# Output products of 288 columns, no masked tail copy and another order of the front, in a kernel that runs a recurrent transformer beside full attention

## The chip, the cores and the metric

The kernel runs on one core of a Trainium2 chip as one program. The metric is the device time of one execution in microseconds (us). Before the change four runs gave 1446.75 to 1453.47 us, with a median of 1451.26 us. Engine names are those of the profile: PE (TensorE, matrix products; PEld is its weight load), DVE (VectorE), ACT (ScalarE), POOL (GpSimd) and SP (SyncE, which here only issues transfers).

## The reference

Two branches read the same input `x` of 2048 tokens with 576 values. Branch A goes through 64 segments of 32 tokens, one after the other, and hands a memory of 8 rows from each segment to the next. Branch B is ordinary attention with 32 heads of 18 values. A gate mixes them.

```python
def _A_ref(x, mem0, Wq, Wk, Wv, Wo, seg_len):       # 32 heads of 128 values, M = 8
    mem = mem0
    for s in range(n_seg):
        h = concatenate([mem, x[:, s * 32:(s + 1) * 32, :]], axis=1)      # 40 rows
        q, k, v = (einsum('btd,dhe->bhte', h, W) for W in (Wq, Wk, Wv))
        scores = where(mask, einsum('bhqe,bhke->bhqk', q, k) * scale, -1e9)
        o = einsum('bhqk,bhke->bhqe', softmax(scores), v)
        o = einsum('bhte,hed->btd', o, Wo)
        mem = o[:, :8, :]
        outs.append(o[:, 8:, :])
g = sigmoid((x * gate_w).sum(-1, keepdims=True))
return g * A(x) + (1 - g) * B(x)                       # B: softmax(q k^T) v wo
```

## The kernel before

**An order written by a planner.** Nothing runs in the order of the source. Each piece of work is an operation added with `add(name, engines, duration, function, dependencies, priority, ...)`; a list scheduler (`Plan.run`, `Plan.choose`) places all of them on PE, DVE, ACT, POOL and SP from stored durations, priorities (`RANKS`) and a list of numbers that disturb them (`TURNS`, one number for each segment), and the instructions are then emitted in that order, which is fixed from then on. Some operations may go to either of two engines. Where PE would have nothing to do, the planner puts in four empty products as filler (`warm`, L891). It also charges PE for instruction blocks of 128 pairs of weight load and matmul (`fetched`). Buffers, PSUM banks among them, are tokens: four banks, `pb`, are shared by all products except the scores of the first three heads of a visit of attention (`sb`) and the attention outputs (`ob`).

**The front.** 16 tiles of `x` (128 tokens each) are loaded (L577), every second by SP, the others by ACT. The 576 values are cut into four blocks of 144, each of which gives 128 values to a main part and 16 to a tail; the four tails together are 64 values, which are copied twice side by side (`xd`, L586). PE transposes each tile in five pieces (L594, L595) into one bank `ptx`. Three copies empty it: 512 columns by DVE (L605), the lower 64 rows of the tail by ACT (L609), and the segment's last rows of the upper 64 by ACT (L613) into `xL`; POOL gathers the rest of `xL` (L621, L625). `wb`, the projection weights of B, comes by SP (L638, L639), after POOL has cleared its tail rows (`zwb`, behind five `kch` buffers). Then follow the projections of B: `pq` (L726, 36 blocks of 512 tokens), `pvb` (L765, 32 blocks), the gate `pgs` (L805). Their results go to SBUF (`stg`, `vt`; six buffers each) and by SP to DRAM (`qtd`, `ktd`, `vgd`), from where attention reads them back. `xtd`, the transposed input, is stored by SP (L689, L690) in two transfers for each quarter. The weights of the recurrence, `wv`, `wq` and `wk`, come in 12 loads by POOL (L661, L666), each of which is held back until a certain evacuation of the projections is done (`beats`, a list of numbers in `load_weights`; a one-element memset on DVE, L648, is the sign).

**Attention of B.** 512 visits: scores of four heads (L921; `sb`, `sp`), exponentials on ACT (L930, L934), products with the values (L944, `ob`). They are laid beside everything else; 48 may run ahead of the segments, the others are spread over them.

**A segment of A.** The 40 rows are split: 32 (8 of memory and 24 of `x`) go through the chain below, and the projections of the last 8, which no memory enters, are made ahead for 16 segments at once (`last_unit`, L1014, L1018). `ht` holds the transposed rows: four main blocks and two for the tails, number 4 with the tails in partitions 0 to 63 and zeros above, number 5 the other way round, because `wq_t`, `wk_t` and `wv_t` hold two halves of the heads in the two halves of the partitions. The chain of a segment is: six projections `pvv` (L1270), evacuation `tm` (L536 on DVE, L534 on ACT: one helper, `copier`), transposes by DMA, `qk` (L1370), scores `psh` (L1385, L1393), exponentials (L1403), sums `pss`, reciprocals, `prb` (L1437), `pso` (L1459), copies `ot` (L536, L534), and the output product `acc` (L1178). All of it is done in two halves of 16 heads. The output product lays the four blocks of 144 output columns in the four column groups of PE: for each head four matmuls of 32 columns of `ot` by 144 columns of `wo`. Both halves add to one bank. Then the step to the next segment: `obf`, the cast of 128x144 (L1491); `bd` (L1494), the 16 tail columns of each block, repeated and multiplied by a block mask; the fold `pw` (L1513, L1516), small products with pieces of the identity that turn the 8 memory rows into columns; and `ht` (L1526). The late 8 rows of four segments have an output product of their own (`last_out`, 128 matmuls from `otl`), a cast `lbf` (L1553) and a store to `a_dram`.

**The end.** The last products of B (L1682, L1686) are combined with A's rows, read back from `a_dram`, and stored.

Of the kernel before, what the change touches and what calls it, by code (L numbers as in the profile page):

```python
# [57 lines left out]
    4631337, 8646187, 1378870, 7501440, 2920177, 4654182, 7605534, 9845851, 5556687, 7848165, 8138688,  # L58
    4164138, 9631951, 8743530, 8517736, 8416788, 8054394, 26198, 4924923, 6020877, 419892, 4069693, 9961447,
    272705, 2067139, 5598403, 4732882, 1549104, 2438338, 4732220, 2816846, 6717326, 0, 4595530, 1604277,  # L60
    3301672, 3391804, 6451070, 1335116, 2191429, 1816650, 137719, 3868929, 6979129, 7748565, 6565385, 6695724,
    3839835, 1101164, 2930722, 1706253, 5558244, 8554903, 5450599, 6671946, 1219286, 8487400, 306976, 914519,
    2736263, 2428798, 8437421, 1579326, 8783738, 2627635,
# [47 lines left out]
class Plan:  # L111
# [7 lines left out]
    CROWDED = (28.0, 125.0)  # L119
# [256 lines left out]
def kernel(  # L376
# [29 lines left out]
    QC = 512  # L406
# [40 lines left out]
    sel = const.tile([P, M], BF16, name="sel")  # L447
    bmask = const.tile([P, NF, TR], BF16, name="bmask")
# [10 lines left out]
    nc.vector.memset(bmask[:], 0.0)  # L459
# [11 lines left out]
    for j in range(4):  # L471
        r = slice(32 * j, 32 * j + 32)
        nc.vector.tensor_copy(out=sel[r, :], in_=ident[r, 32 * j:32 * j + M])
        nc.vector.memset(bmask[r, j, :], 1.0)
    selm = ident[:, :].rearrange("p (j t) -> p j t", t=32)[:, :, 0:M]
# [3 lines left out]
    xtd = dpool.tile([Dm, S], BF16, name="xtd")  # L479
# [66 lines left out]
    nc.vector.memset(xT[TL:P, NF, :], 0.0)  # L546
# [4 lines left out]
    z_wb = zero("zwb", wb[TL:P, NF, :], 1.6, 0.05)  # L551
    z_xl = [zero("zxl0", xL[TL:P, NF, :], 0.5, 0.2), zero("zxl1", xL[0:TL, NF + 1, :], 0.5, 0.2)]
# [20 lines left out]
    def x_tile(n):  # L573
        def load(e):
# [5 lines left out]
            f"x{n}", "SP" if n % 2 == 0 else "ACT", 0.42, load, prio=0.1, take=("xn",), dmas=1, kb=147  # L580
        )

        def dup(e):
            box["xd", n] = xd = given(pw, "xd", [P, 2, NF, TR], BF16)
            tail = box["xn", n][:, :].rearrange("p (c r) -> p c r", r=RW)[:, :, P:RW]
            nc.vector.tensor_copy(out=xd[:, :, :, :], in_=tail.unsqueeze(1).to_broadcast([P, 2, NF, TR]))  # L586
# [3 lines left out]
        def turn(e):  # L590
            box["ptx", n] = ptx = bank([P, NF + 1, P], BF16, "ptx")
            xn, xd = box["xn", n], box["xd", n]
            for c in range(NF):
                nc.tensor.transpose(out=ptx[:, c, :], in_=xn[:, RW * c:RW * c + P], identity=ident[:, :])  # L594
            nc.tensor.transpose(  # L595
                out=ptx[:, NF, :], in_=xd[:, :, :, :].rearrange("p a c r -> p (a c r)"), identity=ident[:, :]
# [7 lines left out]
            f"xe{n}", "DVE", psum_copy(512, True),  # L604
            lambda e: nc.vector.tensor_copy(out=xT[:, 0:NF, cols], in_=box["ptx", n][:, 0:NF, :]), [tu], prio=0.2,  # L605
        )
        e2 = add(
            f"xf{n}", "ACT", act_time(128),
            lambda e: nc.scalar.copy(out=xT[0:TL, NF, cols], in_=box["ptx", n][0:TL, NF, :]), [tu], prio=0.2,  # L609
        )  # L610

        def third(e):
            nc.scalar.copy(  # L613
                out=xL[TL:P, NF + 1, lc].rearrange("p (s t) -> p s t", t=LO),
                in_=box["ptx", n][TL:P, NF, :].rearrange("p (s t) -> p s t", t=seg)[:, :, last],
            )

        e3 = add(f"xg{n}", "ACT", act_time(32), third, [tu, e1, e2, *z_xl], prio=0.2, give=(("pb", tu, 0),))

        def gather(e):  # L620
            nc.gpsimd.tensor_copy(  # L621
                out=xL[:, 0:NF, lc].rearrange("p c (s t) -> p c s t", t=LO),
                in_=xT[:, 0:NF, cols].rearrange("p c (s t) -> p c s t", t=seg)[:, :, :, last],
            )
            nc.gpsimd.tensor_copy(  # L625
                out=xL[0:TL, NF, lc].rearrange("p (s t) -> p s t", t=LO),
                in_=xT[0:TL, NF, cols].rearrange("p (s t) -> p s t", t=seg)[:, :, last],
            )

        e4 = add(f"xl{n}", "POOL", 0.6, gather, [e1, e2, *z_xl], prio=2.0)  # L630
        xdone.append((e1, e2, e3, e4))
# [4 lines left out]
    def load_wb(c):  # L636
        def fn(e):
            dma(out=wb[:, c, :], in_=rows(B_wqkv, c))  # L638
            dma(out=wb[TR * c:TR * c + TR, NF, :], in_=B_wqkv[RW * c + P:RW * c + RW, :])  # L639

        return add(f"wb{c}", "SP", 0.8, fn, [z_wb], prio=0.14, dmas=2, kb=500)

    wbl = [load_wb(c) for c in range(NF)]
    beats, weight_loads, paced = [], {}, []

# [8 lines left out]
    def load_weights():  # L654
        k = 0
        for w, src, name in ((wv, A_Wv, "wv"), (wq, A_Wq, "wq"), (wk, A_Wk, "wk")):
            w2 = src.rearrange("d h e -> d (h e)")
            weight_loads[name] = []
            for c in range(NF):
                def load_w(e, w=w, w2=w2, c=c):  # L660
# [3 lines left out]
                    for two in range(2):  # L664
                        o = TL * two + TR * c
# [6 lines left out]
                    behind(f"{name}{c}", beats[(12, 16, 18, 23, 26, 30, 34, 38, 43, 48, 53, 57)[k]], lambda w=w, c=c: w[0][0:1, 0, c, 0:1], 3, load_w, [], 3.0)  # L672
# [3 lines left out]
    def load_gw(e):  # L676
        for c in range(NF):
            nc.gpsimd.dma_start(out=gw[:, c:c + 1], in_=gate_w[RW * c:RW * c + P].unsqueeze(1))
            nc.gpsimd.dma_start(
                out=gw[TR * c:TR * c + TR, NF:NF + 1], in_=gate_w[RW * c + P:RW * c + RW].unsqueeze(1)  # L680
            )

    gwl = add("gw", "POOL", 8.0, load_gw, [wbl[-1]], prio=0.9, tail=3.0)

    def store_xt(q):
        c4 = slice(q * QC, (q + 1) * QC)

        def fn(e):
            dma(out=xtd[0:NF * P, c4].rearrange("(c p) t -> p c t", p=P), in_=xT[:, 0:NF, c4])  # L689
            dma(out=xtd[NF * P:Dm, c4], in_=xT[0:TL, NF, c4])  # L690

        deps = [o for n in range(4 * q, 4 * q + 4) for o in xdone[n][:2]]
# [1066 lines left out]
```

## Time and profile before

| what | us |
|---|---|
| median of four runs | 1451.26 |
| the profiled execution | 1453.47 |
| its span, first to last instruction | 1451.7 |
| first projection `pvv` of segment 0 starts | 162.7 |
| first and last `obf` start | 184.5, 1420.7 |
| ACT: exponentials of B (L930, L934) | 743.6 and 305.0 |
| DVE: `tm`, `ot`, `obf`, `bd` (L536, L536, L1491, L1494), one | 0.689, 0.484, 0.307, 0.196 |

A row of the profile names the line, the engine, the operation and "out<-in" by the program's names. "Idle before" is what the engine spent waiting ahead of such an instruction, and the name behind the arrow is what ended that wait; "issue" is a wait for nothing that the profile shows. A timeline row with x16 is 16 instructions that follow each other.

### The profile page before, as it was taken

To read this page: it belongs to the slowest core of one execution; us is meant where nothing else is said; L and a number is where in the kernel's file an instruction comes from. 1 tells how busy PE (TensorE), PEld (TensorE's weight loads), DVE (VectorE), ACT (ScalarE), POOL (GpSimd) and SP (SyncE) were. 2 spreads that over 40 slices of the span, in tenths; PEclk is the share of its full clock that TensorE was granted. 3 is DMA by queue.
4 is the path that set the end of the run, shared out by engine and by line. 5 is a ranking of instruction groups with operands and counts; after the bars stand their busy time and mean duration, and the time that the engine had idled before them with its cause. 6 is when DMAs were issued, how large, how long until landed. Compare 5 with 4: busy or idle time off the path is not lost. (4 is left out here: it accounts for less than half of the span.)

```text
span 1451.7 us, 79317 instructions
## 1 busy us (share of the span) xinstructions
PE 1353.8 (93%) x35682; PEld 747.6 (52%) x35682; DVE 786.6 (54%) x1873; ACT 1094.2 (75%) x1302; POOL 537.6 (37%) x1166
## 2 busy tenths in 40 slices
PE   6789999999999999999999999999999999989998
PEld 4334545555555545555555445555554444444545
DVE  6334555565555455555555554545565554555556
ACT  1357799878788777787777786788769887778884
POOL 5233254334532355322453325343344334421320
PEclk9899999999999999999999999999999999999999
DMA  6895633233333443423333333433334333433335
GB/s 213 274 319 168 154 77 77 59 68 70 87 57 68 59 80 76 72 62 61 79 67 72 66 63 69 76 59 74 62 71 94 53 54 58 69 61 54 53 71 177
DMA packets 343424, 130.79 MB, mean 90 GB/s; under 512 B 296943, under 2 KB 329159, under 8 KB 343083
## 3 DMA queue, kind: packets, MB, share of 16 engines
q1 hardware_dynamic: 314771, 81.20, 28.5%
q0 software_dynamic: 27088, 43.31, 10.7%
q8 instruction: 279, 4.57, 1.3%
q10 hardware_dynamic: 1224, 1.20, 0.3%
q14 instruction: 62, 0.51, 0.1%
HBM read 52.74 MB, written 30.86 MB: 58 GB/s over the span
## 5 line engine op out<-in xcount | busy, mean ns | idle before, releaser
L930 ACT ACTIVATE etb<-sb 128x1536 bf16<-128x1536 f32 x512 | 743.6, 1452 | 229.2 <-PE sp L921 166.1
L536 DVE CAST tm<-pvv 128x512 bf16<-128x512 f32 x343 | 236.4, 689 | 238.3 <-PE pvv L1270 235.5
L1270 PEld LDWEIGHTS <-ht 128*32 128x32 bf16 x7680 | 197.6, 97 | 222.8 <-issue 37.8
L934 ACT ACTIVATE etb<-sp 128x512 bf16<-128x512 f32 x512 | 305.0, 596 | 0.0
L921 PE MATMUL sb<-qch,kch 32*128 32x512 bf16 x1536 | 202.0, 385 | 8.4 <-ACT etb L930 4.1
L944 PE MATMUL ob<-etb,vch 128*32 128x512 bf16 x2048 | 199.5, 384 | 0.3 <-DVE tq L972 0.3
L921 PE MATMUL sp<-qch,kch 32*128 32x512 bf16 x512 | 196.9, 385 | 0.5 <-issue 0.2
L1178 PE MATMUL acc<-wo,ot 128*32 128x144 bf16 x8192 | 169.8, 228 | 15.5 <-issue 12.4
L1178 PEld LDWEIGHTS <-ot 128*32 128x32 bf16 x8192 | 135.3, 97 | 48.9 <-issue 27.0
L1270 PE MATMUL pvv<-wk_m,ht 128*32 128x512 bf16 x2048 | 145.7, 381 | 2.0 <-DVE vl L536 0.7
L1270 PE MATMUL pvv<-wq_m,ht 128*32 128x512 bf16 x2048 | 142.6, 381 | 3.7 <-DVE ht L1526 1.8
L1270 PE MATMUL pvv<-wv_m,ht 128*32 128x512 bf16 x2048 | 144.5, 380 | 0.0
L921 PEld LDWEIGHTS <-kch 32*128 32x128 bf16 x2048 | 55.7, 91 | 144.2 <-issue 122.1
L536 DVE CAST ot<-pso 128x320 bf16<-128x320 f32 x203 | 93.5, 484 | 66.9 <-PE pso L1459 63.5
L1221 POOL COPY ht<-xg 128x96 bf16<-128x96 bf16 x64 | 17.9, 280 | 282.3 <-PE pvv L1270 273.5
L1370 DVE COPY qk<-tt 128x512 bf16<-128x512 bf16 x256 | 77.6, 308 | 39.0 <-DMA tt<-tm 36.3
L840 POOL DMA_DIRECT2D qch<-qtd x120 | 61.1, 516 | 75.6 <-PE sp L921 66.5
L1403 ACT ACTIVATE et<-psh 128x320 bf16<-128x320 f32 x128 | 56.5, 444 | 35.1 <-PE psh L1393 30.7
L1448 DVE TENSOR_TENSOR et<-et,prb 128x320 bf16<-128x320 bf16 x128 | 61.4, 484 | 37.2 <-PE prb L1437 31.8
L840 POOL DMA_DIRECT2D otd<-stage x124 | 62.9, 514 | 45.9 <-DVE stage L987 32.4
L944 PEld LDWEIGHTS <-vch 128*32 128x32 bf16 x2048 | 54.1, 95 | 44.7 <-issue 34.7
L840 POOL DMA_DIRECT2D kch<-ktd x112 | 57.0, 516 | 44.6 <-PE sp L921 37.0
(169 smaller groups left out, 1934.2 us busy)
## 6 DMA issues: line engine op xcount, KB each, us to landing
xl<-qkd SPq DMA_DIRECT2D x64, 128.0 KB
v_sb<-tm SPq DMA_DIRECT2D x256, 32.0 KB
qkd<-vl POOLq DMA_DIRECT2D x48, 128.0 KB, 2.1
wo<-in_A_Wo_dram POOLq DMA_DIRECT2D x4, 1152.0 KB
vgd<-vt SPq DMA_DIRECT2D x32, 128.0 KB
wv_m<-in_A_Wv_dram POOLq DMA_DIRECT2D x4, 1024.0 KB, 7.2
wq_m<-in_A_Wq_dram POOLq DMA_DIRECT2D x4, 1024.0 KB
wk_m<-in_A_Wk_dram POOLq DMA_DIRECT2D x4, 1024.0 KB, 8.3
```

What stands on the lines that cost most here:

```text
L536: nc.vector.tensor_copy(out=out_of(), in_=in_of())
L840: dma(out=rows_, in_=pads) if out else dma(out=pads, in_=rows_)
L921: nc.tensor.matmul(sb[:, j, :] if j < 3 else sp[:, :], lhsT=kc[r, o:o + P], rhs=qt_[r, :], start=True, stop=True, tile_position=(32 * j, 0),)
L930: nc.scalar.activation(out=etb[:, 0:3, :], in_=box["sb", gq, kb][:, :, :], func=ACT.Exp, scale=scale_b)
L934: nc.scalar.activation(out=etb[:, 3, :], in_=box["sp", gq, kb][:, :], func=ACT.Exp, scale=scale_b)
L944: nc.tensor.matmul(ob[32 * j:32 * j + 32, :], lhsT=vc[:, o + 32 * j:o + 32 * j + 32], rhs=etb[:, j, :], start=(kb == 0), stop=(kb == NKB - ...
L1178: nc.tensor.matmul(acc[32 * j:32 * j + 32, :], lhsT=o[:, slot, t0:t0 + CT], rhs=wo[:, h, RW * j:RW * j + RW], start=(first and s_ == 0), s ...
L1221: nc.gpsimd.tensor_copy(out=ht[:, 0:NF, M:CT], in_=xg[:, 0:NF, t])
L1270: nc.tensor.matmul(pv[32 * j:32 * j + 32, :], lhsT=ht[:, cc, :], rhs=rw, start=(c == 0), stop=(c == NF), tile_position=(0, 32 * j), skip_g ...
L1370: eng.tensor_copy(out=opened["qk"][:, hf, a, 0:16 * L].rearrange("p (j i t) -> p j i t", i=4, t=L)[:, :, :, 0:CT], in_=box["tt", s, a, hf] ...
L1403: nc.scalar.activation(out=opened["et", hf][:, :], in_=box["psh", s, hf][:, :], func=ACT.Exp, scale=scale_a)
L1448: nc.vector.tensor_tensor(out=et[:, :], in0=et[:, :], in1=box["prb", s, hf][:, :], op=ALU.mult)
```

## The change

There are four parts, and an order planned anew for all of them.

1. **Output products.** `out_pieces` gets `wide`. Then a head has two matmuls of 288 columns instead of four of 144; heads with an even number write the partitions 0 to 63, those with an odd number 64 to 127. So the bank holds two partial sums, which `halved` adds: two copies of 64x144 to an FP32 tile `sum` (DVE or ACT) and two additions (DVE). It is used for the first half of each segment and for the late rows. The second half stays at 144 columns, has a bank of its own, and `obf` becomes the addition of that bank and `sum`. The four output blocks lie in the order 0, 2, 1, 3 (`SL`).
2. **Tails.** The tails are laid out so that each block has its 16 values twice (32 partitions). `bd` is gone; the fold takes the tail columns from `obf` itself, which is made 16 columns wider, always as 12 matmuls, and the zeros come from multiplying by `keep` when `pw` is evacuated. `xtd` and `xg` carry the doubled tails, so that a transfer each replaces two and three.
3. **Front.** One copy (DVE or ACT) empties `ptx`, and POOL makes the tails of `xL` with two multiplications. The four `sel` copies and the memset of `xT` are gone. The four main loads of `wb` are shared by SP and ACT, ahead of most tiles of `x`.
4. **Later transfers.** The recurrence weights wait for later beats, and the stores of `xtd` wait for beats 60, 63, 65 and 67 (of 68).

```diff
 TURNS = [
-    4631337, 8646187, 1378870, 7501440, 2920177, 4654182, 7605534, 9845851, 5556687, 7848165, 8138688,
+    2111328, 67141, 7494148, 5731960, 1836367, 3235203, 8807839, 6809858, 7066401, 7875931, 2541338, 4628007,
...
-    CROWDED = (28.0, 125.0)
+    CROWDED = (40.0, 112.0)
...
-        nc.vector.tensor_copy(out=sel[r, :], in_=ident[r, 32 * j:32 * j + M])
-        nc.vector.memset(bmask[r, j, :], 1.0)
-    selm = ident[:, :].rearrange("p (j t) -> p j t", t=32)[:, :, 0:M]
+        nc.vector.memset(keep[r.start:r.start + TR, NF:NF + 1], 1.0)
...
+    SL = (0, 2, 1, 3)
...
-    nc.vector.memset(xT[TL:P, NF, :], 0.0)
...
-    z_wb = zero("zwb", wb[TL:P, NF, :], 1.6, 0.05)
+    z_wb = zero("zwb", wb[:, NF, :], 1.6, 0.05)
...
         e1 = add(
-            f"xe{n}", "DVE", psum_copy(512, True),
-            lambda e: nc.vector.tensor_copy(out=xT[:, 0:NF, cols], in_=box["ptx", n][:, 0:NF, :]), [tu], prio=0.2,
+            f"xe{n}", ("DVE", "ACT"), (psum_copy(640, True), act_time(640)),
+            copier(lambda: xT[:, :, cols], lambda: box["ptx", n][:, :, :]), [tu], prio=0.2, give=(("pb", tu, 0),),
         )
...
     def load_wb(c):
-        def fn(e):
-            dma(out=wb[:, c, :], in_=rows(B_wqkv, c))
-            dma(out=wb[TR * c:TR * c + TR, NF, :], in_=B_wqkv[RW * c + P:RW * c + RW, :])
-
-        return add(f"wb{c}", "SP", 0.8, fn, [z_wb], prio=0.14, dmas=2, kb=500)
+        main = add(
+            f"wb{c}", "SP" if c % 2 == 0 else "ACT", 0.42,
+            lambda e: (nc.sync if e == "SP" else nc.scalar).dma_start(out=wb[:, c, :], in_=rows(B_wqkv, c)),
+            [z_wb], prio=0.12, dmas=1, kb=442,
+        )
...
+    BEATS = (20, 24, 27, 30, 33, 36, 40, 45, 49, 53, 57, 60)
...
-                    behind(f"{name}{c}", beats[(12, 16, 18, 23, 26, 30, 34, 38, 43, 48, 53, 57)[k]], lambda w=w, c=c: w[0][0:1, 0, c, 0:1], 3, load_w, [], 3.0)
+                    behind(f"{name}{c}", beats[BEATS[k]], lambda w=w, c=c: w[0][0:1, 0, c, 0:1], 3, load_w, [], 3.0)
...
+    XBEATS = (60, 63, 65, 67)
...
-            dma(out=xtd[0:NF * P, c4].rearrange("(c p) t -> p c t", p=P), in_=xT[:, 0:NF, c4])
-            dma(out=xtd[NF * P:Dm, c4], in_=xT[0:TL, NF, c4])
+            dma(out=xtd[:, c4].rearrange("(c p) t -> p c t", p=P), in_=xT[:, :, c4])
...
-                    for j in range(4):
+                    for j in range(2 if wide else 4):
+                        q = 2 * (s_ % 2) + j if wide else j
+                        n, d = (2 * RW, 2 * RW * j) if wide else (RW, RW * SL[j])
                         nc.tensor.matmul(
-                            acc[32 * j:32 * j + 32, :], lhsT=o[:, slot, t0:t0 + CT],
-                            rhs=wo[:, h, RW * j:RW * j + RW],
...
+                            acc[32 * q:32 * q + 32, :], lhsT=o[:, slot, t0:t0 + CT], rhs=wo[:, h, d:d + n],
...
+    def halved(name, state, done, out_of, last_give, prio, held=()):
...
+                copier(
+                    lambda: state["sum"][64 * i:64 * i + 64, :],
+                    lambda: state["acc"][64:128, RW * i:RW * i + RW],
+                )(e)
...
+                nc.vector.tensor_tensor(
+                    out=out_of()[r, :], in0=state["acc"][0:64, RW * i:RW * i + RW], in1=state["sum"][r, :], op=ALU.add,
+                )
...
-            nc.gpsimd.tensor_copy(out=ht[0:TL, NF, M:CT], in_=xg[0:TL, NF, t])
-            nc.gpsimd.tensor_copy(out=ht[TL:P, NF + 1, M:CT], in_=xg[TL:P, NF + 1, t])
+            for k in (NF, NF + 1):
+                nc.gpsimd.tensor_tensor(
+                    out=ht[:, k, M:CT], in0=xg[:, NF, t], in1=keep[:, k:k + 1].to_broadcast([P, CT - M]), op=ALU.mult
+                )
...
-        def ob_bd(e, s=s):
             nc.vector.tensor_tensor(
-                out=opened["bd"][:, 1, :].rearrange("p (c r) -> p c r", r=TR),
-                in0=box["obf", s][:, P:RW].unsqueeze(1).to_broadcast([P, NF, TR]), in1=bmask[:, :, :], op=ALU.mult,
-            )
...
+                out=opened["obf"][:, s % 4, 0:RW], in0=st["acc"][:, :], in1=st0["sum"][:, :], op=ALU.add
+            )
...
+        c1 = add(f"oc{s}", "DVE", 0.308, ob_cast, [mids[1], half_sum], prio=0.3, take=("obf",) if s % 4 == 0 else (),
```

In the built order the pairs of weight load and matmul on PE go from 35,682 to 32,813: 2,048 products `acc` fewer from `ot`, 1,024 fewer from `otl`, 90 more in the fold, 116 more as filler. DVE has 118 and ACT 42 of the new copies to `sum`, DVE all 160 additions. Of the 512 visits of attention 35 instead of 37 stand ahead of the first projection of segment 0.

## The prediction

> **What bounds the kernel now.** The page's first part is read first.
>
> ```profile
> PE 1353.8 (93%) x35682; PEld 747.6 (52%) x35682; DVE 786.6 (54%) x1873; ACT 1094.2 (75%) x1302; POOL 537.6 (37%) x1166
> ```
>
> PE carries the span. The share hides where it stands still, so the same row is read by stage (columns: window, length, busy us of each engine with its instructions, granted clock, DMA share, GB/s).
>
> ```profile
> 0.00:20.00 20.00, 8.46 (x63) 6.48 (x64) 14.51 (x41) 5.97 (x25) 17.12 (x51) 1.00 0.69 218
> 20.00:40.00 20.00, 16.53 (x97) 9.72 (x97) 9.39 (x25) 1.24 (x3) 6.89 (x21) 1.00 0.72 225
> 40.00:60.00 20.00, 14.83 (x139) 8.61 (x138) 6.05 (x14) 4.22 (x12) 4.76 (x12) 0.74 0.88 287
> 60.00:120.00 60.00, 52.27 (x357) 22.54 (x355) 26.94 (x54) 34.90 (x36) 22.30 (x40) 1.00 0.85 274
> 120.00:162.00 42.00, 40.98 (x508) 24.91 (x505) 17.62 (x35) 33.34 (x35) 10.19 (x21) 1.00 0.62 194
> 162.00:1420.00 1258.00, 1194.87 (x34209) 657.46 (x34201) 691.40 (x1663) 1003.97 (x1179) 476.36 (x1024) 1.00 0.36 69
> 1420.00:1452.00 32.00, 25.81 (x328) 17.90 (x324) 20.66 (x44) 10.57 (x13) 0.00 (x0) 1.00 0.46 150
> ```
>
> Three stages follow: a front up to the first projection of segment 0 (162.7 us), 64 segments of 19.62 us (first and last `obf` at 184.5 and 1420.7, 63 steps), and an end of 31 us. PE idles 20.2 us in the first 60, with a clock of 0.74 in the last 20 of them, and 63 us in the segments. There I looked at what it waits for, in the timeline of PE.
>
> ```profile
> 889.62 0.36 PE L1178 MATMUL acc<-wo,ot 128*32 128x144 bf16 x12
> 891.78 0.25 PE L1178 MATMUL acc<-wo,ot 128*32 128x144 bf16 x4 [1.80 <-issue]
> 891.84 0.35 PE L1437 MATMUL prb<-ident,rq 128*32 128x128 bf16 x12
> ```
>
> An output product stops after 12 of its 16 matmuls, which wait for no semaphore. The page's DMA part has the reason:
>
> ```profile
> q8 instruction: 279, 4.57, 1.3%
> ```
>
> These are 279 packets of 16,384 bytes: PE's 71,364 instructions at 64 bytes, 128 weight-load-and-matmul pairs a packet. Between 184 and 1420 us consecutive packets start at least 3.23 us apart, a quarter of them within 3.71. I added up every matmul that ends over 0.12 us later than its predecessor's end plus its own columns (0.42 ns a column, from 512 columns every 215 ns), with no semaphore before it: 48 stalls, **29.4 us**, 21.0 of them at L1178; 45 of the 48 end 1.2 to 2.0 us after a packet has landed. So PE's instruction stream runs dry where many short pairs come close together. Last, the step from one segment to the next, on PE and DVE:
>
> ```profile
> 896.90 0.39 PE L891 MATMUL ob<-unit,nil 128*32 128x512 bf16 x4
> 897.27 0.20 PE L1516 MATMUL pw<-ident,obf 128*32 128x32 bf16 x4
> 897.49 0.21 PE L1516 MATMUL pw<-sel,bd 128*32 128x8 bf16 x8
> ...
> 896.90 0.31 DVE L1491 CAST obf<-acc 128x144 bf16<-128x144 f32 x1 [2.06 <-PE acc L1178]
> 897.25 0.19 DVE L1494 TENSOR_TENSOR bd<-obf,bmask 128x64 bf16<-128x64 bf16 x1
> 897.77 0.21 DVE L1526 CAST ht<-pw 128x48 bf16<-128x48 f32 x1 [0.33 <-PE pw L1516]
> ```
>
> Cast, masked copy, fold, cast: from the last `acc` matmul to the next `pvv` 1.26 us on average, and PE fills it with empty matmuls (L891). This chain, not PE's work, sets that step.
>
> **Part by part.** The sum is made against the profiled execution, 1453.47 us (span 1451.7 and 1.8 around it); the median of the four runs is 1451.26.
>
> *Front.* These lines carry it.
>
> ```profile
> 1.36 2.60 DVE L473 COPY sel<-ident 32x8 bf16<-32x8 bf16 x1
> 8.23 0.29 PE L595 MATMUL ptx<-ident,xd 128*128 128x128 bf16 x1 [3.82 <-DVE xd L586]
> 9.34 0.43 SPq L638 DMA_DIRECT2D wb<-in_B_wqkv_dram  x1
> 20.65 1.88 PE L765 MATMUL pvb<-wb,xT 128*128 128x288 bf16 x7 [0.85 <-DMA wb<-in_B_wqkv_dram]
> 42.41 2.52 PE L765 MATMUL pvb<-wb,xT 128*128 128x288 bf16 x10 [5.23 <-ACT vt L534]
> ```
>
> The four `sel` copies and the `xT` memset hold DVE until 7.9 us: gone. `wb` is issued from 9.3 us, behind five tile loads on SP; in the changed order SP issues two tiles, then the four tails and two `wb`, ACT the other two, and their memset stands first on POOL (1.53 us, over by 3.1 instead of 5.5). 1.99 MB at the 300 GB/s of 10 to 20 us is 6.6 us, so the products can run without a wait from near 13 instead of 20.65 us: 6 to 7 us, since two of them ran before. The 5.2 us at 37 and the 2.8 at 53 us end on `vgd` and `kch` transfers that share the DMA engines with three 0.6 MB `xtd` stores and the first `wv` load; both are moved later (the stores behind beats 60 to 67, past all but the last q and k stores on SP). That and the lost clock (14.83 busy at 0.74, 3.9 us) make a ceiling of 18. Against it: the 14.2 MB of recurrence weights now come in a shorter stretch beside the second half of the v stores, and PE already lost 4.8 us there, at 90, 95 and 99 us, to `vt` evacuations that waited for `vgd`. The loads' 36 issues on POOL (0.81 us for a main block, 0.49 for a tail) stand later and closer, ahead of the first `vch`, `qch` and `kch` loads there, of which one waited 3.3 us before; no visit of the front needs these so early. The copy of a transposed tile costs little on either engine (0.47 us for 512 columns on DVE, plus 0.26 and 0.18 on ACT, become one of 0.6 to 0.7) and it lies beside transfers. The first `pvv` now stands behind 35 visits instead of 37, which come back later. Between 0 and −18 I take **−10**.
>
> *Output products.* Four 144-column matmuls end every 62.4 ns, four of 512 every 215; by the line between, four of 288 take 122.3. The first half of a segment falls from 16 × 62.4 to 8 × 122.3 ns, 0.02 us, the late rows of four segments by 0.04: 64 × 0.02 + 16 × 0.04 = **−1.9**. Columns are what PE spends, and their number stays.
>
> *Instruction stream.* The built order has 32,813 pairs instead of 35,682, 491 a segment instead of 535. 128 narrow pairs take 2.0 us of PE against 3.5 to 3.75 for the next packet, short by 1.6; the new 96 (32 wide, 64 narrow) take 1.98 against 2.6 to 2.8, short by 0.7; the late rows' 64 wide ones take 1.96 against 1.8, short by nothing. So 57% of L1178's 21.0 goes, 12, and one more from the other lines: **−13**, between 0 and −29.4. The Trainium skill ("Runtime: NRT & Kernel Launch", Instruction fetch mechanics) says that crossing a 16 KiB block is mostly hidden. By that rule this term would be 0 and the sum 1437; the 1.80 us row decides for me.
>
> *The tail copy and the halves.* `bd` goes: 0.196 and 0.036 of gap, 63 times, −14.6; the fold stays at 12 short matmuls, and the multiply in its evacuation costs what the copy did (a two-input DVE row of 320 columns has 484 ns, a copy 484). Added: `obf` now waits for the first half's sum, two copies and two adds of 64x144 (0.30 each by the 307 ns of `obf` and the 297 of `lbf`). In the trace of before, `obf` starts 1.58 us after the second `ot` copy, 0.33 of it stalls counted above: 1.25. DVE's order mostly has the four behind that copy: 4 × 0.31 + 0.1 = 1.35, later by 0.10, 6.3 us in all. 42 of the 160 copies stand on ACT, among exponentials of 1.45 us; that may add as much as 0.1 a copy, 4.2. So −14.6 + 10.5 = **−4.1**, between −14.6 and +28 (0.45 us a segment). Queued behind the waiting `obf` on DVE are the next casts of `tm`, for which the transposes wait; on PE the fold and the next `pvv`. Two halves hold two PSUM banks of four instead of one; PE's waits for a bank there are small (`psh` on ACT `etb` 1.9, on DVE `et` 1.8, on DVE `vl` 1.3 us in all), so nothing is charged.
>
> *The rest.* POOL's two products a segment in place of two copies (0.23 us) lie inside its 273 us of waiting for `pvv`. DVE gets about 1 us a segment, mostly inside the 94 us that it waits for `acc`. The order has 29 more groups of empty matmuls; they stand in idle time. At the end a 2.3 us stall may go and the halves add up to 1.2: **−0.5**.
>
> Sum: −10 − 1.9 − 13 − 4.1 − 0.5 = −29.5; 1453.5 − 29.5 = **1424**.
>
> **The rivals.** *The front gives nothing*: DMA, at 0.85 to 0.95 from 40 to 110 us, only moves its waits to the later weights. For it: the crowded rows; against: the idle 5 to 10 us, where DMA ran at 82 GB/s. 1434. *The stalls stay*: the stream runs dry elsewhere. For it: 8.4 us of the stalls are at other lines. 1437. *Everything lands*: front −18, stalls −21, tail −8.3: 1404. *The order undoes it*: all places were drawn anew, with 29 more fillers: no change, 1451. *Slower*: the sum of the halves becomes the end of each segment. At 0.484 us an instruction instead of 0.30 (the 320-column row) the four take 1.99 after the copy, 0.74 over the products' 1.25, and `obf` itself 0.18 more: 63 × 0.92 = 58 against the other terms' 40, 1471. It decides from 0.64 us a segment. Against it: the 144-column rows.
>
> **How the numbers follow.** Forecast 0.40, front nothing 0.20, stalls stay 0.15, everything lands 0.13, order 0.05, slower 0.07. The range 1404 to 1445 leaves out half of "everything lands" and the last two, 0.18. Faster by over 0.3% (4.4 us, about what runs of this kernel can tell): 0.88; within: 0.05; slower: 0.07.
>
> **What would show it.** Right: first `pvb` without a wait near 13 us, first `pvv` near 150; "issue" at the output line under half; `obf` within 0.2 us of the last `acc`; segments near 19.3 us. Wrong: `obf` waiting for `sum` rather than `acc`; PE idle behind `vgd` between 60 and 110; new instruction stalls at `psh` or `prb`.

## The result, and the profile after

53 runs of the changed kernel gave a median of 1445.85 us (1441.56 to 1454.13), 79 runs of the kernel before 1450.97 us. The ratio is 0.9965, 95% interval 0.9955 to 0.9975: faster by 5 us, where 27 were forecast, and 0.85 us above the range. The profiled execution took 1443.84 us with a span of 1442.1, 9.6 less than the span of before.

The page's first part and its row of instruction packets come first.

```profile
PE 1352.9 (94%) x32813; PEld 722.2 (50%) x32813; DVE 852.6 (59%) x2074; ACT 1103.7 (77%) x1310; POOL 528.0 (37%) x1146
...
q8 instruction: 256, 4.19, 1.2%
```

PE is as busy as before, DVE has 66 us more. The same row by stage (columns as in the prediction):

```profile
0.00:20.00 20.00, 7.01 (x46) 4.87 (x47) 4.69 (x28) 3.47 (x5) 16.22 (x48) 1.00 0.72 202
20.00:40.00 20.00, 20.00 (x154) 12.18 (x152) 12.78 (x31) 7.83 (x10) 7.72 (x36) 1.00 0.47 147
40.00:60.00 20.00, 13.49 (x87) 5.17 (x85) 5.84 (x14) 7.76 (x8) 5.35 (x9) 0.89 0.72 226
60.00:120.00 60.00, 55.18 (x425) 24.03 (x425) 27.89 (x56) 36.09 (x38) 25.78 (x45) 0.96 0.94 321
120.00:164.00 44.00, 36.45 (x426) 25.74 (x423) 14.54 (x30) 20.35 (x23) 8.84 (x18) 0.88 0.61 196
164.00:1412.00 1248.00, 1194.69 (x31428) 632.52 (x31425) 764.96 (x1872) 1016.66 (x1215) 464.12 (x990) 1.00 0.37 69
1412.00:1442.00 30.00, 26.04 (x268) 17.73 (x264) 21.90 (x47) 11.51 (x13) 0.00 (x0) 0.99 0.50 170
```

**The front gained nothing.** From 20 to 40 us PE has no gap now, and the first visit of attention starts at 32.1 instead of 52.5. But the first `pvv` starts at 164.6 (162.7 before), the first `obf` at 184.9 (184.5): the last row before the segments shows PE busy 36.45 of 44 us at a clock of 0.88, where before it was 40.98 of 42 at 1.00. The timeline of PE and DVE has the places.

```profile
15.93 0.66 PE L763 MATMUL pvb<-wb,xT 128*128 128x288 bf16 x2 [4.37 <-DMA wb<-in_B_wqkv_dram]
...
57.13 2.29 PE L724 MATMUL pq<-xT,wb 128*128 128x512 bf16 x5 [5.17 <-DVE wv_m L646]
...
152.16 0.69 DVE L539 CAST vl<-pv 128x512 bf16<-128x512 f32 x1 [6.34 <-DMA qkd<-vl]
...
152.91 0.58 PE L1013 MATMUL pv<-xL,wk_m 128*128 128x128 bf16 x4 [4.14 <-DVE vl L539]
```

At 57 us the mark `wv_m` (the sign on DVE) stands behind an evacuation to `stg` that waited 7.43 us for a `qtd` store. At 152 the buffers `vl` wait for their `qkd` stores, which run beside the four loads of `wo` (issued from 137 to 158 us, 1152 KB each), and PE waits for `vl`. The kernel before had the same two kinds of transfer there, and PE without a gap (19.99 us busy from 140 to 160). Two things differ in the profiles. The second and third `wo` loads follow each other within 1.2 us instead of 8.1 (first before, then changed):

```profile
137.65 0.90 POOL L1115 DMA_DIRECT2D wo<-in_A_Wo_dram  x1 [0.65 <-DVE ht L1155]
145.77 0.88 POOL L1115 DMA_DIRECT2D wo<-in_A_Wo_dram  x1 [7.21 <-DVE wo L648]
```

```profile
144.36 0.92 POOL L1114 DMA_DIRECT2D wo<-in_A_Wo_dram  x1
145.53 0.90 POOL L1114 DMA_DIRECT2D wo<-in_A_Wo_dram  x1 [0.25 <-DVE wo L646]
```

And nine visits of attention stand between 140 us and the first `pvv` before, but only one in the changed kernel, whose visits run earlier; so PE has little else to do there while it waits. No run tells the two apart.

**The segments gained 9 us.** First to last `obf` is now 1227.3 us, 63 steps of 19.48 (19.62 before). By the criterion of the prediction, the stalls without a semaphore fell from 29.4 us in 48 places to 1.9 in 3. One step, in the timeline of DVE and then of PE:

```profile
892.99 0.89 DVE L539 CAST ot<-pso 128x320 bf16<-128x320 f32 x2 [0.47 <-PE pso L1497]
893.91 0.65 DVE L539 COPY sum<-acc 64x144 f32<-64x144 f32 x2
894.59 0.63 DVE L1215 TENSOR_TENSOR sum<-acc,sum 64x144 f32<-64x144 f32 x2
895.31 0.31 DVE L1530 TENSOR_TENSOR obf<-acc,sum 128x144 bf16<-128x144 f32 x1
896.02 0.21 DVE L1556 TENSOR_TENSOR ht<-pw,keep 128x48 bf16<-128x48 f32 x1 [0.40 <-PE pw L1548]
```

```profile
893.11 1.66 PE L1182 MATMUL acc<-wo,ot 128*32 128x288 bf16 x80
...
895.67 0.22 PE L1544 MATMUL pw<-ident,obf 128*32 128x32 bf16 x4 [0.25 <-DVE obf L1530]
```

The products end at 894.77, `obf` starts at 895.31: it waits for the four operations on the halves, which follow the last `ot` copies without a gap. The groups between 185 and 1400 us say the same for all steps; first the kernel before, then the changed one (after the bar: idle before, and what ended it).

```profile
L1178 PE MATMUL acc<-wo,ot 128*32 128x144 bf16 x7936 | 164.5, 228 | 14.8 <-issue 12.1 <-DVE ot L536 1.7
...
L1491 DVE CAST obf<-acc 128x144 bf16<-128x144 f32 x62 | 19.0, 307 | 95.0 <-PE acc L1178 92.8 <-DMA qch<-qtd 2.2
```

```profile
L1182 PE MATMUL acc<-wo,ot 128*32 128x288 bf16 x1984 | 86.2, 288 | 3.1 <-issue 0.6 <-DVE ot L539 0.5
...
L1530 DVE TENSOR_TENSOR obf<-acc,sum 128x144 bf16<-128x144 f32 x63 | 19.4, 307 | 13.8 <-PE acc L1182 9.1
...
L1544 PE MATMUL pw<-ident,obf 128*32 128x32 bf16 x252 | 14.0, 189 | 9.6 <-DVE obf L1530 8.6
```

"Issue" at the output line went from 12.1 to 0.6. DVE no longer idles ahead of `obf`: it is late itself, and PE waits for it at the fold. Cut into legs, from the records of all steps:

| leg of a step | before, us | after, us | times 63 |
|---|---|---|---|
| first `pvv` to last `pso` | 15.96 | 16.08 | +7.4 |
| to the end of the last `ot` copy | 0.85 | 0.92 | +4.5 |
| to the end of the last `acc` | 1.54 | 1.08 | −28.7 |
| to the start of `obf` | 0.06 | 0.30 | +15.4 |
| to the end of `ht` | 1.14 | 0.96 | −11.5 |
| to the next `pvv` | 0.07 | 0.13 | +4.3 |

40 us of gains and 32 of losses. By kind of step: the 15 with late rows fell from 20.90 to 19.77 us, the other 48 rose from 19.22 to 19.39.

### The profile page after: what moved, and what is told of

It reads as the page before. It is cut to its first block, busy times and chain, and to the rows that moved or that the text cites. A ratio compares the mean times of both kernels' runs of the same rounds, so it can differ in the third digit from the quotient of the medians.

```text
span 1442.1 us, 73805 instructions
## 1 busy us (share of the span) xinstructions
PE 1352.9 (94%) x32813; PEld 722.2 (50%) x32813; DVE 852.6 (59%) x2074; ACT 1103.7 (77%) x1310; POOL 528.0 (37%) x1146
## 5 line engine op out<-in xcount | busy, mean ns | idle before, releaser
L539 DVE CAST tm<-pvv 128x512 bf16<-128x512 f32 x348 | 239.4, 688 | 232.8 <-PE pvv L1309 230.0
L1309 PEld LDWEIGHTS <-ht 128*32 128x32 bf16 x7680 | 201.2, 96 | 221.4 <-issue 43.1
L1182 PE MATMUL acc<-wo,ot 128*32 128x288 bf16 (+1 forms) x6144 | 163.0, 247 | 4.9 <-DVE ot L539 2.1
L539 DVE CAST ot<-pso 128x320 bf16<-128x320 f32 x220 | 100.6, 484 | 66.1 <-PE pso L1497 63.3
L1182 PEld LDWEIGHTS <-ot 128*32 128x32 bf16 x6144 | 112.3, 97 | 43.2 <-DVE ot L539 20.3
L1278 POOL COPY qk<-xl 128x256 bf16<-128x256 bf16 x128 | 50.0, 403 | 67.4 <-PE psh L1431 38.9
```

What stands on the lines that cost most here:

```text
L539: nc.vector.tensor_copy(out=out_of(), in_=in_of())
L1182: nc.tensor.matmul(acc[32 * q:32 * q + 32, :], lhsT=o[:, slot, t0:t0 + CT], rhs=wo[:, h, d:d + n], start=(first and s_ == (s_ % 2 if wide ...
L1278: nc.gpsimd.tensor_copy(out=opened["qk"][:, f, :, 0:16 * L].rearrange("p a (h t) -> p a h t", t=L)[:, :, :, CT:L], in_=box["xlt", s][:, :, ...
L1309: nc.tensor.matmul(pv[32 * j:32 * j + 32, :], lhsT=ht[:, cc, :], rhs=rw, start=(c == 0), stop=(c == NF), tile_position=(0, 32 * j), skip_g ...
```

## The experiments

Each run keeps the planned order of the kernel that it starts from: only what an operation issues is edited, not its stored duration, so the planner places everything as it did (e7 alone changes the order). Ratios are to the kernel before on the same chip, where its median was 1457.6 us (e1 to e4), 1464.7 (e5 to e8), 1459.7 (e9 to e12) and 1462.2 (e13 to e16). The changed kernel itself was run again in e5 alone (0.9947). e13, which is the changed kernel with 64 products more, had 0.9904. So the ratio of nearly the same kernel moves by 0.2 to 0.6% (3 to 9 us) from one of these four groups of runs to another, and differences within a group are the safer ones. Theory A is that the sum of the halves ends each segment, B that the new order does, C that the front's gain went to transfers that meet later.

**e1, no sums.**

```diff
         def low(i):
             def fn(e):
+                if name[0] == "u":
+                    return
...
-                out=opened["obf"][:, s % 4, 0:RW], in0=st["acc"][:, :], in1=st0["sum"][:, :], op=ALU.add
+            nc.vector.tensor_copy(out=opened["obf"][:, s % 4, 0:RW], in_=st["acc"][:, :])
```

> The changed kernel in its own order of instructions, with the four operations on the first half's bank (two copies, two additions) left out in all 64 segments, and obf a cast of the second half's bank alone: the first 16 heads' share of the output is missing; the late rows keep their sums. Theory A (the sum of the halves ends each segment): in the changed kernel obf starts on average 0.30 us after the last acc against 0.06 before, so 63 x 0.245 = 15 us come back; obf again 0.05 us behind acc, segments near 19.2 us, time near 1430 (1423 to 1435). Theory B (the new order of the work, its visits and fillers, sets the segment, and the wait for the sum stands beside it): segments within 0.06 us of 19.48 and the time within 4 us of the changed kernel's 1446.

Ratio 0.9845 (0.9818 to 0.9873), segments 19.21 us, `obf` 0.05 us behind `acc` on average (0.12 at most). Its group between 185 and 1400 us:

```profile
L1534 DVE CAST obf<-acc 128x144 bf16<-128x144 f32 x64 | 19.7, 308 | 77.0 <-PE acc L1182 75.3 <-DMA a_dram<-lbf 1.6
```

DVE waits for the products again, 77 us. Against the changed kernel's 0.9965 this is 17 us. Against e4 on the same chip, which has the segments of the changed kernel (19.59 us) and a front up to 4 us earlier, it is 12. This is theory A, and B falls.

**e2, the tail copy put back.**

```diff
+            nc.vector.tensor_tensor(out=opened["bdx"][:, :]..., in0=opened["obf"][:, s % 4, P:RW]...,
+                in1=keep[:, 0:1]..., op=ALU.mult)
```

> The changed kernel in its own order, with a DVE operation of the size of the old bd (128x64 from 16 columns of obf) put back between obf and the fold, whose tail products read it. My prediction's term: 0.196 us and 0.036 of gap come back 63 times, +14.6 us, segments 19.71, time 1460. Rival (the step from obf to the next pvv has slack that PE fills with visits and empty products): less than half of it, time below 1453.

Ratio 1.0031 (1.0008 to 1.0054), 9.6 us over the changed kernel by the ratios. From `obf` to the end of `ht` it has 1.19 us instead of 0.96: the 0.23 is there, and two thirds of the 14.6 are seen in the time; against e4 on the same chip, the legs from `obf` to the next `pvv` have 0.19 us a step more, 12 us. The copy was on the path.

**e3, narrow first halves.**

```diff
-        def piece(lo):
+        def piece(lo, wide=wide and name[0] == "l"):
...
+                if name[0] == "u":
+                    if i == 0:
+                        copier(lambda: state["sum"][:, :], lambda: state["acc"][:, :])(e)
+                    return
```

> The changed kernel in its own order, with the first half of each segment again as 64 products of 144 columns in a bank of its own, and one copy of 128x144 to sum in place of two copies and two additions. The late rows keep 288 columns, the computation is whole. PE gets 2,048 more pairs. If the number of pairs makes the instruction stalls, they return at the output line: 15 to 25 us without a semaphore against 0.9, and the shorter chain of the halves (three DVE operations fewer) gives back at most the 15 us of theory A: time 1445 to 1457. If the stalls went away for another reason (the new places of the work), they stay under 5 us, and the time falls to 1430 to 1435 by theory A or stays at 1446 by theory B.

Ratio 1.0031 (1.0005 to 1.0057). `obf` is 0.06 us behind `acc`, and 26.0 us of stalls are back in 44 places. So the 288 columns in the segments are worth their sums, by some 10 to 15 us in this order (against the 0.9965, and against e4 on the same chip).

**e4, `wo` early.**

```diff
+        for q in range(4):
+            nc.gpsimd.dma_start(out=opened["wo"][:, 8 * q:8 * q + 8, :], in_=A_Wo[...]...)
```

> The changed kernel in its own order, with the four loads of wo (4.7 MB in all) issued by POOL as soon as the space is there, near 118 us, not at 137 to 157; their marks on DVE go. Theory C (the front's gain was lost between 140 and 160 us, where the wo loads share the DMA engines with the qkd stores, whose vl tiles PE then waits for: PE busy 12.6 of 20 us at a clock down to 0.50): PE busy at least 17 of 20 us there, the first pvv at 152 to 159 instead of 164.6, the time 1435 to 1441. Rival D (the loads only move the wait to the vld stores at 119 to 133 us, or the first pvv waits for something else): first pvv within 2 us of 164.6, the time within 4 us of 1446.

Ratio 0.9926 (0.9897 to 0.9954). The loads were issued from 130.7 us only: their space is that of `xT`, and the last `xtd` store, moved late by the change and issued at 126.0, still read it. PE was busy 14.8 of 20 us from 140 to 160, where 17 were expected, and the first `obf` came at 182.9. The unedited front of e1, e2 and e3 gave 187.0, 185.6 and 183.0, so 0 to 4 us: in favour of C, but small.

**e5, the changed kernel again.** 

> The changed kernel as it is, as the base for the other runs on this chip: a ratio of 0.9965 to the kernel before, first pvv between 162 and 167, segments 19.5 to 19.6 us.

Ratio 0.9947 (0.9923 to 0.9971), first `pvv` 161.7, segments 19.63 us: this profile is slower in the segments by 0.15 us a step than the first one of the same kernel, so steps are compared within a chip.

**e6, one copy.**

```diff
-                copier(lambda: state["sum"][64 * i:64 * i + 64, :], lambda: state["acc"][64:128, RW * i:RW * i + RW])(e)
+                    copier(lambda: state["sum"][64:128, :], lambda: state["acc"][64:128, :])(e)
```

> The changed kernel in its own order, with one copy of 64x288 to sum in place of two of 64x144; the two additions stay, the computation is whole. A copy of 64x144 took 0.310 us, one of 128x320 0.484; between them one of 288 columns is 0.45, so the chain of the halves is shorter by 0.17 us. Theory A (the sum ends the segment): about half of the segments wait for it longer than that, so 5 to 8 us off the changed kernel on the same chip. Theory B (the order sets the segment): within 3 us of it.

Ratio 0.9845 (0.9809 to 0.9881), 1442.0 us beside 1454.4 of e5 and 1464.7 of before. Its DVE timeline in the same segment:

```profile
891.09 0.89 DVE L539 CAST ot<-pso 128x320 bf16<-128x320 f32 x2 [0.47 <-PE pso L1495]
892.01 0.46 DVE L539 COPY sum<-acc 64x288 f32<-64x288 f32 x1
892.51 0.64 DVE L1212 TENSOR_TENSOR sum<-acc,sum 64x144 f32<-64x144 f32 x2
893.24 0.31 DVE L1528 TENSOR_TENSOR obf<-acc,sum 128x144 bf16<-128x144 f32 x1
```

From the `ot` copies to `obf` 1.26 us instead of 1.43. `obf` waits 0.20 us behind `acc` on average (0.30 in e5), and the segment is 19.38 us instead of 19.63. From the last `ot` copy to `obf` it is 0.095 us a step, 6 us, as expected; 8 us more are in the leg from `pvv` to `pso`, 16.09 instead of 16.22, which was not.

**e7, other numbers for the order.** Only `TURNS` differs, those of the kernel before from the second number on.

> The changed kernel with the numbers TURNS of the kernel before for the 64 segments; the first number, which orders the front, stays. The work is the same, only the places in the segments differ. If the new order hides a gain of the change (theory B, and my rival that the order undoes it), this one gives segments under 19.4 us. By theory A the wait for the sum stays in any order that was not made to avoid it: acc to obf still over 0.2 us on average and segments of 19.5 to 20.0 us.

Ratio 1.1095 (1.1052 to 1.1137), 1624 us, 39 us of stalls, `obf` 0.67 us behind `acc`, and 2,128 empty products put in by the planner instead of 700. The wait for the sum stays, as A expects, but the segments, at 21.80 us, are far over both forecasts: these numbers, found for the one kernel, were worth nothing in the other, and the run cannot tell what the new order alone cost. What a part of the change does alone is therefore asked in a fixed order.

**e8, `wo` late.**

```diff
+                if q == 0 and kind == 1 and b > 3:
+                    nc.sync.dma_start(out=opened["wo"][:, r, :], in_=A_Wo[r]...)
```

> The changed kernel in its own order, with the four loads of wo issued by SP, one after each of the last four qkd stores of the first group, near 155 to 165 us, so that the earlier stores of 139 to 155 us have the DMA engines to themselves. Theory C (these stores, slowed by the loads, hold the vl tiles and so PE): PE busy 17 or more of the 20 us from 140 to 160, clock over 0.9, first pvv 5 to 10 us earlier than the changed kernel's on the same chip; how much of it stays depends on the first acc, which needs all four loads. Rival D (the qkd stores are slow by themselves): PE there 12 to 14 of 20 us again, first pvv within 2 us.

Ratio 0.9927 (0.99 to 0.9953). By stage, and then DVE in its timeline:

```profile
140.00:160.00 20.00, 18.86 (x326) 15.74 (x326) 10.10 (x20) 7.17 (x11) 2.35 (x6) 1.00 0.50 158
160.00:180.00 20.00, 9.89 (x176) 3.90 (x172) 5.42 (x13) 7.38 (x8) 1.99 (x6) 0.66 1.06 234
```

```profile
172.72 0.29 DVE L1411 COPY qk<-tt 128x512 bf16<-128x512 bf16 x1 [11.23 <-DMA tt<-tm]
```

Without the loads beside the stores PE works through 140 to 160 (12.3 us in e5), and the first `pvv` comes at 156.2 instead of 161.7: C is right about the cause. But now the loads meet the first segment's transposes `tt`, for which DVE waits 11.2 us (0.7 in e5), and the first `obf` comes at 187.2 (183.0 in e5): nothing stays.

**e9, the kernel before with wide late rows alone.**

```diff
+        wide = name[0] == "l"
...
-                nc.vector.tensor_copy(out=obf[:, :], in_=st["acc"][:, :])
+                for i in range(2):
+                    nc.vector.tensor_copy(out=obf[64 * i:64 * i + 64, :], in_=st["acc"][64:128, RW * i:RW * i + RW])
+                for i in range(2):
+                    nc.vector.tensor_tensor(out=obf[r, :], in0=st["acc"][0:64, ...], in1=obf[r, :], op=ALU.add)
```

> The kernel before in its own order, with one part of the change alone: the late rows (one set for four segments) as 64 products of 288 columns, and two copies and two additions in place of the cast lbf. By segments, 23.8 of the 29.4 us of stalls of the kernel before lie in the 16 steps that hold the late rows, which took 20.9 us against 19.2 for the others. Theory S (the 128 narrow pairs of the late rows beside the segment's own make the stalls): 5 to 9 us of stalls stay, the steps with late rows take 19.3 to 20.0 us, the time falls by 13 to 23 us, ratio 0.984 to 0.991. Rival (the segments' own 128 narrow pairs make them, 2,048 of which were taken away by the change): over 15 us of stalls stay, ratio over 0.994.

Ratio 1.0076 (1.0058 to 1.0094): slower. 17.7 us of stalls stay, in 28 places, and many have moved: 4.9 in the steps with late rows (24.2 before) and 12.7 in the others (5.1 before). Theory S fell: the stalls went from its steps, but the time rose by 11 us. The rival has the numbers without the reason: the segments' own narrow pairs were there before too, and had few stalls outside those steps. What else made the time longer, three more DVE operations for each set of late rows among it, is not told apart.

**e10, narrow late rows in the changed kernel.** The same switch as in e3, with `name[0] != "l"`, and one cast to `lbf`.

> The changed kernel in its own order, with the late rows again as 128 products of 144 columns and one cast; the segments keep their 288 columns. Theory S: 12 to 24 us of stalls come back, most of them in the steps with late rows, time 8 to 20 us over the changed kernel, less what three DVE operations less, 16 times, give. Rival (the segments' first halves made the stalls go): under 6 us of stalls, time within 4 us of the changed kernel or below it.

Ratio 1.0055 (1.0031 to 1.0079), 13 us over the changed kernel by the ratios; 21.0 us of stalls, 17.3 of them in the steps with late rows, which take 20.46 us beside 19.5 for the others. As expected; but as in e3 and e9 every later pair has also moved in the blocks of 128.

**e11, the front's stores early.** The edit of e4, and the `xtd` stores moved behind v stores.

```diff
+            for q in {(0, 7): [0], (0, 11): [1], (0, 15): [2, 3]}.get((hf, kb), ()):
+                dma(out=xtd[:, c4].rearrange("(c p) t -> p c t", p=P), in_=xT[:, :, c4])
```

> The changed kernel in its own order, with the four xtd stores issued right after v stores near 38 to 52 us, not at 102 to 124, and the wo loads by POOL as soon as their space is there: in the run with wo early the loads started at 129.5 us, when the last xtd store (issued at 126) had read the xT that they overwrite. Now they can start near 118 us, and use the DMA engines from 120 to 137, where they were 0.41 busy. Theory C: PE busy 17 or more of 20 us from 140 to 160, first pvv at 153 to 159 us, first obf at 174 to 179 against 183 to 185, and the time 6 to 9 us under the changed kernel's on the same chip. Rival: the stores hold up the qtd and vgd stores at 40 to 60 us, and the start of segment 0 stays within 2 us.

Ratio 0.9924 (0.9898 to 0.995), first `pvv` 159.8, first `obf` 179.7 (162.4 and 183.5 in e10 on this chip): both just later than theory C expected.

```profile
40.00:60.00 20.00, 12.15 (x75) 4.70 (x74) 4.10 (x10) 7.76 (x8) 3.58 (x6) 0.90 1.01 316
60.00:80.00 20.00, 16.58 (x91) 5.98 (x93) 7.53 (x15) 9.65 (x10) 7.14 (x12) 0.85 0.89 275
80.00:100.00 20.00, 16.68 (x135) 9.13 (x134) 9.31 (x25) 11.59 (x13) 5.36 (x9) 1.00 0.95 326
...
140.00:160.00 20.00, 19.82 (x331) 17.62 (x332) 9.73 (x19) 9.36 (x12) 5.81 (x14) 1.00 0.41 127
```

The gap at 140 is closed (19.82 of 20 us, 12.30 in e10), and more than half of that comes back at 40 to 100: 45.4 us busy there, 49.7 in e10. 4 us of the front stay.

**e12, that front and the single copy.** 

> The run before it and the single copy of 64x288 together: the single copy alone had a ratio of 0.9845 to the kernel before, 15 us under the changed kernel on the same chip. If the two do not touch each other, 0.979 to 0.981; if the front gives nothing, 0.984 to 0.985.

Ratio 0.9826 (0.9801 to 0.9851), 1436.0 us beside 1459.7: the best of all versions. Between the two forecasts; its interval holds the 0.9845 of e6, so how much the front adds is not settled.

**e13 and e14, the blocks shifted.** The same edit in the changed kernel and in the one before, ahead of segment 0:

```diff
+        for _ in range(64):
+            nc.tensor.transpose(out=ptm[:, 0, M:2 * M], in_=box["m0"][0:M, 0:P], identity=ident[0:M, 0:M])
```

> The changed kernel in its own order, with 64 small transposes of 8 columns more on PE ahead of segment 0 (2 to 4 us there), whose result is not read. The instructions of the segments are the same, but lie 64 pairs later in the blocks of 128. Theory P (the order was planned on the blocks' places: a block's end in a run of short pairs makes the stall, wherever it comes): stalls in the segments go from 1 to 8 us up to 10 to 25, and the time rises by as much beside the 2 to 4. Theory N (there are few enough pairs in a segment now): the stalls stay under 9 us, the time within 5 us of the changed kernel.

> The kernel before in its own order, with the same 64 transposes ahead of segment 0. Theory P: the stalls leave the steps with late rows (23.8 of 29.4 us there) and come up in others, 35 to 60 us in all, ratio 1.008 to 1.025. Theory N: about 29 us as before, ratio 1.002 to 1.004 for the transposes alone.

The changed kernel: 3.9 us of stalls in 12 places, ratio 0.9904 (0.9872 to 0.9937), which is 6 to 9 us below the unshifted kernel's 0.9947 and 0.9965; why it is lower is open. The kernel before: 46.1 us in 71 places, ratio 1.0277 (1.0241 to 1.0312), segments 20.36 us. The steps with late rows keep 21.2 us of these stalls, which P did not expect; the other steps have 24.8 instead of 5.1. The output group of each, e13 first:

```profile
L1184 PE MATMUL acc<-wo,ot 128*32 128x288 bf16 x1984 | 87.0, 289 | 2.5 <-DVE ot L539 0.7
```

```profile
L1180 PE MATMUL acc<-wo,ot 128*32 128x144 bf16 x7646 | 163.2, 229 | 20.5 <-issue 17.7 <-DVE ot L536 1.6
```

So each theory holds for one kernel, at this one shift. The planner fitted the order of the kernel before to the places of the blocks, and its 29.4 us were already the fitted figure. In the changed kernel, with fewer pairs, the place hardly matters. e3, e9 and e10 lie between, at 18 to 26 us, with places that nothing was fitted to; a new order for them was not tried.

**e15, the copy on ACT.** `nc.scalar.copy` in place of `copier` in e6. 

> The single copy of 64x288 to sum, always on ACT (0.394 us there, 0.461 on DVE), at its place in the order. DVE, behind its ot copies, has two additions less to wait for than four operations, but the copy may wait for an exponential of 1.45 us. Theory A: if ACT is free within 0.2 us of the first half's end, the wait of obf goes below 0.1 us and the ratio below 0.983; if it mostly waits behind an exponential, acc to obf rises over 0.3 us and the ratio over 0.990.

Ratio 0.9979 (0.9953 to 1.0006), `obf` 0.37 us behind `acc`. The additions on DVE, between 185 and 1400 us:

```profile
L1212 DVE TENSOR_TENSOR sum<-acc,sum 64x144 f32<-64x144 f32 x124 | 37.2, 300 | 47.7 <-ACT sum L1206 45.4
```

45 us of waiting for ACT: the second case of the expectation. ACT has the shorter operation and the longer queue.

**e16, the single copy and `wo` early.** 

> The single copy of 64x288 (on the engine of the order) with the wo loads issued as soon as their space is there, the xtd stores at their late places. The one had 0.9845, the other 0.9926 against the changed kernel's 0.9947 and 0.9965: together 0.980 to 0.983, if the few us of the earlier first obf (182.9 against 183 to 187) stay.

Ratio 0.9867 (0.9836 to 0.9899), first `obf` 186.2. The earlier first `obf` did not stay, and the ratio is over the forecast. The changed kernel as it is was not run on this chip then, so what the early `wo` gives beside the copy is not known.

## Why the prediction was wrong

The direction was right; the sum, −29.5, missed in four terms. In the profiled pair the span fell by 9.6.

- **Front, −10: failed.** The first `obf` came 0.4 us later. The idle time that I listed at 20 to 40 us did go. The step that failed is "between 0 and −18 I take −10": I looked for the collision of the moved loads at 90 to 100 us and in POOL's queue, not at the end of the row, where `wo`, which waits for the space of `xT`, lies beside the `qkd` stores, with hardly a visit left there to keep PE busy. Nor did I see the 5.2 us at 57, behind a `qtd` store and a beat. e8 shows that `wo` beside these stores makes the gap at 140, and that taking them apart moves the wait to the next transfers; e11, where 4 us stay, that the DMA engines are nearly full from 40 to 100 us as well. "First `pvb` without a wait near 13 us" was wrong too: `wb` ended waits at 15.9 and 17.0.
- **Output products, −1.9, and instruction stream, −13: too small.** 27.5 of the 29.4 us of stalls went; the leg that ends with `acc` gave 28.7. I judged block by block, by a packet in 3.5 to 3.75 us, and left 0.7 of the 1.6 us of a narrow block standing. e14 and e13 show what counts: at a shift of half a block the kernel before gets 16.7 us of stalls more, the changed one 2.0. The Trainium skill ("Runtime: NRT & Kernel Launch", Instruction fetch mechanics) has the crossing of a block as mostly hidden; in e14 nothing but the place of the blocks in the segments was changed, and 46.1 us of stalls disagree, in e13 3.9 nearly agree.
- **The halves, +10.5: the size was nearly right, its place in the sum was not.** I forecast 1.35 us from the last `ot` copy to `obf`; it was 1.38. But with the stalls gone the products end after 1.08, so the sum is what ends the leg, and 15.4 of the 28.7 us are handed to the wait for it. My sign for "wrong", `obf` waiting for `sum`, is what the profile shows. e1 gives 12 to 17 us for the four operations, e6 takes most of that back with one operation fewer. The rival "slower" had this mechanism; at 0.30 to 0.31 us an operation it was under its deciding point, as the prediction argued.
- **Tail copy, −14.6: somewhat too large.** The leg from `obf` to `ht` gave −11.5, and the next leg took +4.3 back. e2 gives 0.23 us a step for the copy, as forecast, and 10 to 12 us in all.
- **The rest, "DVE gets about 1 us a segment, mostly inside the 94 us that it waits for `acc`": failed.** These 94 us were the very wait that the change took away. The legs up to the last `ot` copy, which I had at nothing, cost 11.9 us. Part hangs on DVE's operations: that leg is 16.08 us in e1 and 16.17 in e2, which has five operations more, on one chip, and 16.09 in e6 against 16.22 in e5 (16.18 in e8, which has the operations of e5). The first profile of the changed kernel, with the operations of e5, had 16.08, so a part of the 11.9 may come from comparing single profiles. The rest is not told apart from the new order, whose 112 more empty products from 185 to 1400 us make PE's busy time there 9.6 us longer (57.2 instead of 47.6).
- **The end, −0.5:** 31.0 to 29.9 us, near enough.

Put together: −28.7 − 11.5 + 15.4 + 4.3 + 11.9 = −8.6 for the segments, 0.4 for the front, −1.1 at the end. (From first to last `obf` it is −8.8; the legs are averages with their own rounding.) "The front gives nothing", at 1434, was right about the front. The rest of the miss lies in the wait for the sum and in the legs up to the last `ot` copy. By its number the nearest rival is "the order undoes it", 1451, but the stalls did go, and e1 and e6 show that the halves took much of it back; how much of the legs up to `ot` is the order's stays open.

## What to carry to other kernels

When an edit removes a wait, ask at once which input of the same instruction is second to arrive, and count the gain only down to it. An engine's waiting time is no room for new work if the change is made to remove that wait. A transfer that is moved must be followed to the transfers it will run beside at its new time, up to the first one that nothing waits for.

## What the runs showed of the hardware

- A shift of all later PE instructions by 64 pairs, half a block, cost the kernel before 2.8% of its time. The stalls without a semaphore rose by 16.7 us, the segments by 47 (about 0.1 us a step of it may be the chip): the criterion, which leaves out every matmul with a semaphore before it, shows only a part of the cost.
- A copy out of a bank has a large fixed part: 64x144 in 0.310 us and 64x288 in 0.461 on DVE, 0.274 and 0.394 on ACT, so half the columns save only about a third of the time. Two copies on DVE joined into one save 0.16 us of 0.62.
- The clock was lower after an idle stretch: PE stood still from 148.8 to 152.9 us in the changed kernel, and the granted clock was 0.61 from 150 to 155 us and 0.50 from 155 to 160; four products of 128 columns took 0.63 us there and 0.39 before.
